# A delta-rule attention with an MLP behind it: the recurrence's small products as 128x64 tiles with two heads stacked

## The chip, the cores and the metric

The kernel runs on one core of one Trainium2 chip. Its time is the device time of one execution in microseconds (us). A core has TensorE (matrix products, PE in the profile, its weight loads PEld), VectorE (DVE), ScalarE (ACT), GpSimd (POOL), SyncE (SP, which here only issues DMAs) and 16 DMA engines. Lines named L960 and the like are lines of the kernel before, unless the text says that they are of the changed one.

## What is computed

q, k, v are [4, 8, 768, 48] and beta [4, 8, 768], all fp32: four batches, eight heads, 768 steps, 48 channels.

```python
k_n = k / (np.linalg.norm(k, axis=-1, keepdims=True) + 1e-06)
state = np.zeros((B, H, D, D))
for t in range(S):
    y[:, :, t] = einsum('bhd,bhde->bhe', q[:, :, t], state)
    v_old = einsum('bhde,bhd->bhe', state, k_n[:, :, t])
    state = state + beta_t * einsum('bhd,bhe->bhde', k_n[:, :, t], v[:, :, t] - v_old)
x = y.transpose(0, 2, 1, 3).reshape(B, S, H * D)
xn = (x - mean(x)) / sqrt(var(x) + 1e-06) * g_ln      # over the 384 channels
out = x + relu(xn @ w_ch1) @ w_ch2                     # 384 -> 1536 -> 384
```

## The kernel before, in words

The sequence is cut into 12 chunks of 64 steps (C = 64). In a chunk, the 32 pairs of batch and head are held as 16 "heads" in the free dimension and two halves of the 128 partitions (`half(e)`), two heads at a time being neighbours (`hp`, `j`: GP = 8 pairs j).

Within a chunk the recurrence is solved in closed form. `gram` and `queries` (L758) make K K^T and Q K^T, a triangular inverse is made for every head (`first_inverse` for chunk 0 by doubling on TensorE, L710 and L725; `rows_inverse` for the others, row by row on VectorE, L843 and L850, in blocks of 32 that `join` puts together with the 32x32 products L881 and L887). Then `recur(c)` does five products with the state S:

- K S (`state(p_2, kt, 0)`, L960 into PSUM tile `two`), which VectorE subtracts from v (L967);
- Q S (the same line into PSUM tile `by`);
- U = inverse times (v - K S) (`prod_u`, L994), copied by ScalarE (L996);
- the state update K^T U (`state_up`, L1011), which VectorE adds to S (L1021; in chunk 0 a ScalarE copy, L1023);
- Y, added to Q S in PSUM (`out_y`, L1001), copied by ScalarE (L1039).

Each of the five is 32 calls of nc.tensor.matmul: for each of the 8 pairs j, four calls on the four 64x64 tiles of the array, with 48 or 64 rows, 64 stationary columns (48 in the update) and 48 moving columns. Chunk 0 has no K S and Q S, and the last chunk no update. For chunk 0 the U product is L977.

Y is then normalized: in chunk 0 by VectorE's bn_stats and bn_aggr, ScalarE's square root, VectorE's reciprocal and a subtract-and-multiply (L1049 to L1061); in later chunks by `ln_act`, with sums that ScalarE accumulates. It is transposed by TensorE (L1095, chunks 0 to 2) or by VectorE and a DMA round trip through DRAM (later ones) and multiplied by g_ln into `xnt`.

The MLP follows: chunk 0 in two halves of 128 tokens (`by_halves`, L1325 and L1340, 128x128 stationary), chunks 1 to 3 with L1299 for the first product, chunks 4 to 11 with `fifteen` (15 block products instead of 18, L1220, operands combined by GpSimd), and the second product from chunk 1 on as `seven` (7 block products instead of 8, L1420). All products are fp32. The weights come as 8-byte words and are converted in the first 100 us by ScalarE, VectorE and GpSimd (L524, L529, L532, L542).

What sets the order: every step is added to a list by `add`, and `emit` issues the steps in the order of the long table ORDER; the costs, due times and priorities written beside the steps are not used by it. `in_this_order` then fixes that order on each engine, and across the DMA queues of SP and ACT. On TensorE, the recurrence of chunk c stands between dense products of the MLP of chunk c - 1 or of the one before it.

Of the kernel before, what the change touches and what calls it, by code (L numbers as in the profile page):

```python
# [16 lines left out]
C = 64  # L17
# [42 lines left out]
6 5 52 49 0 47 8 44 71 9 50 10 57 51 11 29 13 58 325 18 12 63 54 72 7 55 62 53 42 56 245 60 669 410 78 88 36 32 61 77 89 37 74 73 90 14 38 1 69 3 81  # L60
21 2 4 34 82 68 24 15 23 79 76 83 33 95 84 85 80 86 16 20 66 75 91 17 98 92 93 87 96 94 110 100 97 35 116 99 111 70 101 117 48 102 112 118 122 114 115
27 26 19 113 124 30 121 31 120 103 119 125 106 204 104 123 227 132 105 67 25 64 28 126 22 108 246 65 203 107 z 137 128 135 127 40 134 131 133 45 109
46 244 202 207 198 229 138 39 136 129 140 139 130 232 228 141 142 249 215 230 326 144 148 43 143 248 145 233 152 154 247 153 668 147 328 216 205 150
217 250 208 209 199 218 327 155 146 151 420 41 238 149 158 339 210 200 156 236 418 159 206 160 231 157 413 170 161 213 201 409 162 237 223 415 164 163
239 171 225 340 251 165 174 166 252 671 329 168 412 253 169 175 167 176 234 172 254 255 407 186 331 173 235 179 178 180 177 187 330 256 184 257 59 190
183 673 332 337 211 672 182 338 333 258 375 259 260 240 261:263 191 264 380 265 224 185 212 219 266 226 181 192 193 188 221 267 268 349 242 241 269
270 334 271 220 335 272 222 189 336 378 416 243 350 194 411 376 353 419 273 674 385 274 417 377 195 342 196 275 408 355 379 197 357 351 358 276 361
381 214 341 344 277 362 352 383 278 354 363 390 279 280 343 367 382 281 345 384 370 356 368 369 359 388 282 681 360 283 373 675 364 284 670 285 584
365 286 374 287 582 585 288 435 289 682 583 386 436 290 366 586 291 438 809 292 588 437 414 293 346 439 294 347 295 387 587 395 348 371 296 590 589
803 389 440 421 592 591 606 297 593 422 400 298 607 299 391 300 441 301:303 596 304 305 608 597 306 393 594 307 308 609 309 595 310 600 311 312 598  # L70
313 601 314 396 315 604 316 317 599 610 398 318 392 481 602 319 372 394 477 401 611 320 603 605 442 479 397 475 423 676 623 480 476 621 624 402 478
403 612 399 474 627 322 622 323 613 404 628 324 625 321 614 804 473 626 631 948 660 615 808 632 405 443 482 811 635 801 483 629 484 636 810 485 616
486 947 630 488 633 617 487 424 683 489 639 680 490 618 425 491 812 492 493 645 813 494 429 495 427 496 426 646 497 428 634 498 640 430 499 685 500
1094 647 501 432 502 684 431 637 503 433 434 504 814 648 505 815 506 444 951 507 686 508 687 649 509 445 945 1095 510 1096 511 650 946 512 1093 448
513:515 651 449 516 446 451 517 452 638 450 652 447 1209 457 453 643 458 518 1098 653 459 519 1097 460 816 641 454 654 461 520 956 677 462 455 521 944
456 688 642 955 467 678 655 522 1106 463 523 644 1099 689 524 465 1100 957 466 525 468 464 526 802 470 656 469 527 620 849 657 950 528 958 529 853 850
679 530 690 531 532 851 805 533 854 691 534 659 535 859 661 852 536 537 960 855 538:540 820 541 856 542 860 543 952 544 817 953 545:548 861 549 550
662 551 696 663 857 694 862 666 698 876 693 867 858 664 699 877 865 665 806 818 873 555 874 863 552 866 875 554 667 553 871 878 864 700 1108 868 1211
879 869 872 697 406 961 882 695 1258 870 883 560 959 954 884 658 892 885 1210 893 881 886 558 819 889 559 556 807 561 619 909 564 962 894 562 880 910
557 563 821 887 565 895 890 888 566 701 1105 896 702 692 570 911 569 899 568 897 703 567 1268 912 822 704 891 705 1267 898 900 823 917 707 913 918 914  # L80
706 963 919 1270 826 906 915 1216 571 471 824 827 708 472 828 920 709 1271 825 835 924 829 830 901 836 921 710 925 711 837 712 922 713 1217 964 838
714 831 923 1218 715 832 1205 833 572 716 717 1215 935 1101 573 926 575 902 834 927 839 965 907 903 840 936 1220 574 916 904 937 718 841 1259 905 845
719 1552 966 720 843 908 576 844 848 577 721 1109 846 842 968 847 1222 1110 938 580 1221 928 581 722 939 578 949 723 929 579 724 1554 940 1219 998 725
1551 1369 726:728 967 999 941 729 1111 943 730 969 731 1374 1556 732 1206 733 1002 1107 970 734 1370 1112 735 942 1555 736 1004 1003 1204 737 930 1368
738 971 739 1005 1223 1025 1008 931 972 1022 932 1000 740 1261 741 1557 1010 1001 742 1553 743 744 1102 1011 745 1113 973 1103 746 1564 1006 747 975
1023 1104 1009 748 1379 982 974 749 1378 1014 983 750 1373 984 751 976 752 1007 1208 1114 977 753 933 754 978 985 979 1207 1012 1015 986 755 987 756
1115 757 980 1016 989 981 758 1116 1013 759 988 1020 1028 1017 990 760 1558 934 761 1018 762 1021 763 1212 764:766 1041 767 1019 1031 768 1042 769
1032 770 1043 1122 1038 1224 1125 1024 1120 1029 1033 993 1225 1044 1034 1118 1058 1039 1045 992 1035 1026 1046 1036 1265 771 1047 1059 1037 1226 1027
772 1213 774 1266 773 1227 1030 994 1040 1060 991 1048 1260 1381 1066 1061 1117 1123 1049 1062 1119 1067 1262 1121 1050 1214 1063 1124 1068 1064 778
1051 997 779 1069 777 1052 1566 1073 1382 1070 1056 776 1074 1053 1055 775 1071 1383 1075 1065 1072 780 1367 1269 1054 1559 1084 1263 781 1076 782  # L90
1085 1264 783 1077 784 1086 995 996 1078 1126 785 1079 1384 1228 1272 1081 1380 788 786 1057 787 789 1127 2029 1087 1375 1273 1274 1128 1568 1129 1130
1563 1132 1088 1275 1229 1131 790 1080 1133 2031 1089 1134 1135 1230 1663 1280 1569 1090 1385 1136 1137 1371 1138 1278 1139 1281 1140 1091 1141 1142
1092 2033 1233 1143 1279 1372 1144 1570 1145 1082 1146 791 1235 1147 1231 1148 1242 1234 1149 1236 1276 1237 1232 1849 1243 2034 1244 1150 1286 792
1151 1277 1376 1152 1238 1296 1153 1284 1299 1386 1287 1239 1567 1297 1282 1154 1285 1674 1298 1240 794 1155 2035 1156 1290 1565 1283 1157:1159 1288
1291 1160 1245 1676 1246 1161 1305 1289 1387 1241 1303 1247 795 1390 1377 1249 793 1248 796 1250 1162 1306 1850 1302 1388 800 1294 799 1665 1300 1312
1851 1307 1163 1292 1083 1301 1164 1677 1165 1669 1308 1166 1293 1389 1167 1678 798 1313 1295 1673 1309 1304 1664 1391 1315 1253 1310 1316 1168 1311
1251 1332 1314 797 1317 1322 1169 1318 1170 1323 1171 1333 1329 1324 1680 1319 1172 2030 1334 1254 1320 1173 1335 1252 1321 1392 1174 1679 1175 1675
1176 1325 1393 1667 1177 1340 1326 1178 1845 1341 1179 1336 1571 1846 1327 1256 1342 1257 1852 1331 1337 1255 1343 1668 1180 1396 1330 1338 1181 2041
1394 1182 1183 1328 1347 1395 2142 1344 1433 1348 1345 1423 1349 1346 1444 1339 1681 1428 1397 1350 1424 1358 1399 1398 1351 1857 1400 1184 1359 1421
1662 1352 1401 1560 1185 1405 1425 2144 1406 1402 1186 1445 1435 1360 1407 1187 1449 1438 1353 1561 1188 1442 1403 1361 1189 1434 1408 1452 1562 1450  # L100
1429 1409 1404 1362 1190 1430 1410 1446 1451 1426 1412 1363 1411 1427 1448 1572 1364 1453 1437 1413 1447 1191 1439 1454 1573 1192 1436 1193 1440 1456
1670 1194 1431 1455 1195 1458 1441 1574 1457 1432 1461 2028 1459 1416 1671 1422 1465 1460 1414 1354 1462 1463 1417 1672 1666 1471 1464 1415 1355 1468
1466 2043 1357 1682 1443 1469 1198 1196 1472 1477 1356 1473 1200 1474 1853 1467 1478 1859 2045 1480 1576 1479 1475 2040 1581 1470 1496 1365 1481 1483
1497 1578 1484 1482 1199 1498 1419 1490 1485 1197 1420 1499 1476 1366 1486 1491 1500 1487 1201 1510 1501 1738 1492 1580 1502 1683 1582 1488 1493 1523
1579 1489 1516 1511 1418 1577 1524 1503 1583 1494 1517 1504 1203 1684 1495 1525 1861 1505 1518 1512 1202 1526 1860 1519 1854 1728 1506 1727 1527 1520
# [95 lines left out]
def kernel(  # L201
# [20 lines left out]
    FT = DFF // 128  # L222
    GH = 2 * H
    NP = H // 2
    TURNED = 4
    LNPE = 2
    GP = 2 * NP
    FROM, LATER = 4, 6
# [1421 lines left out]
```

## Time and profile before

| | us |
|---|---|
| median of 3 runs | 511.74 (510.79 to 512.89) |
| the profiled execution | 511.19 |
| its span, first to last instruction | 509.5 |
| TensorE busy | 488.8 |
| VectorE, ScalarE, GpSimd busy | 352.1, 249.9, 276.3 |
| L1420, L1220, L1299 as a share of the chain that ended last | 31%, 22%, 9% |
| the small products L960, L994, L1001, L1011 as a share of that chain | 9% in all |

A group's row in the profile gives line, engine, operation, output<-inputs, shapes and count, then busy time in us and the mean ns of one instruction. Matmuls overlap in the pipeline, so the mean of one is longer than the distance between two starts; the chain that ended last, in order of time, gives what each piece adds: start in us, length in us, line and count. A fp32 matmul call shows as two records.

### The profile page before, as it was taken

To read this page: it belongs to the slowest core of one execution; us is meant where nothing else is said; L and a number is where in the kernel's file an instruction comes from. 1 tells how busy PE (TensorE), PEld (TensorE's weight loads), DVE (VectorE), ACT (ScalarE), POOL (GpSimd) and SP (SyncE) were. 2 spreads that over 40 slices of the span, in tenths; PEclk is the share of its full clock that TensorE was granted. 3 is DMA by queue.
4 is the path that set the end of the run, shared out by engine and by line. 5 is a ranking of instruction groups with operands and counts; after the bars stand their busy time and mean duration, and the time that the engine had idled before them with its cause. 6 is when DMAs were issued, how large, how long until landed. Compare 5 with 4: busy or idle time off the path is not lost.

```text
span 509.5 us, 22177 instructions
## 1 busy us (share of the span) xinstructions
PE 488.8 (96%) x9608; PEld 446.4 (88%) x9608; DVE 352.1 (69%) x776; ACT 249.9 (49%) x613; POOL 276.3 (54%) x432
## 2 busy tenths in 40 slices
PE   6866999999999999999999999999999999999996
PEld 3655888689898898899999999999999999999995
DVE  4679887896799638798548998559999456243251
ACT  4688663652464436427334745336554247463230
POOL 5255518416864497549784553581552851455643
PEclk8697599999999999999999999999999999999999
DMA  9987767777365777374874346644354430211001
GB/s 162 326 159 207 176 178 117 104 161 105 61 97 120 188 105 130 75 109 148 168 90 60 83 72 180 124 60 78 73 96 109 100 61 10 66 48 46 18 16 31
DMA packets 196097, 54.99 MB, mean 108 GB/s; under 512 B 186076, under 2 KB 189404, under 8 KB 196000
## 3 DMA queue, kind: packets, MB, share of 16 engines
q1 hardware_dynamic: 189920, 40.58, 41.9%
q10 hardware_dynamic: 3872, 9.83, 5.9%
q0 software_dynamic: 2208, 3.17, 4.3%
q8 instruction: 75, 1.23, 1.0%
q14 instruction: 22, 0.18, 0.1%
HBM read 36.64 MB, written 16.91 MB: 105 GB/s over the span
## 4 chain that ended last, share of the span: by engine, by line
PE 89%; ACT 3%; DVE 3%; DMA 2%; issue 2%; POOL 1%; ACTq 0%; SPq 0%; DVEq 0%; POOLq 0%
PE f L1420 31%; PE f L1220 22%; PE f L1299 9%; PE two L758 4%; PE f L1325 3%; PE f L1340 3%; PE by L1001 3%; PE two L960 2%; PE by L960 2%; PE two L994 2%; PE two L1011 2%; ACT xt L669 1%; DMA gd<-gsb 1%; DMA kr<-in_k_dram 1%; PE by L887 1%
## 5 line engine op out<-in xcount | busy, mean ns | idle before, releaser
L1407 POOL TENSOR_TENSOR h_all<-h_all 128x256 f32<-128x256 f32 x123 | 90.2, 742 | 132.9 <-PE f L1420 103.8
L1420 PE MATMUL f<-w_sb,h_all 128*128 128x192 f32 x492 | 109.6, 331 | 0.0
L1420 PE MATMUL f<-words,h_all 128*128 128x192 f32 x396 | 86.1, 330 | 0.2 <-POOL h_all L1407 0.2
L1420 PEld LDWEIGHTS f<-w_sb,h_all 128*128 128x128 f32 x492 | 81.9, 190 | 1.6
L1240 DVE TENSOR_TENSOR h_all<-h_all,f 128x512 f32<-128x512 f32 x96 | 63.6, 683 | 19.6 <-PE f L1220 15.6
L850 DVE TENSOR_TENSOR xb<-xb,tmp 128x87 f32<-128x87 f32 (+21 forms) x186 | 74.0, 398 | 4.5
L843 DVE TENSOR_TENSOR tmp<-xb,gb 128x87 f32<-128x87 f32 (+21 forms) x186 | 72.3, 389 | 4.6
L1420 PEld LDWEIGHTS f<-words,h_all 128*128 128x128 f32 x396 | 66.8, 190 | 1.6 <-POOL h_all L1407 0.9
L349 POOL DMA_DIRECT2D tb<-in_k_dram x64 | 41.9, 660 | 14.0 <-DVE kt L738 10.0
L1299 PE MATMUL f<-xnt,w_sb 128*128 128x256 f32 x216 | 49.4, 382 | 0.0
L1242 ACT ACTIVATE h_all<-h_all 128x512 f32<-128x512 f32 x48 | 28.9, 623 | 40.7 <-DVE h_all L1240 40.3
L1299 PEld LDWEIGHTS f<-xnt,w_sb 128*128 128x128 f32 x216 | 40.3, 190 | 5.6
L1236 ACT COPY h_all<-f 128x512 f32<-128x512 f32 x48 | 26.5, 588 | 31.5 <-PE f L1220 20.4
L1438 DVE TENSOR_TENSOR o<-f,x 128x192 f32<-128x192 f32 x33 | 11.6, 355 | 36.8 <-PE f L1420 27.0
L1220 PE MATMUL f<-words,w_sb 128*128 128x128 f32 x256 | 32.5, 277 | 0.1
L1220 PEld LDWEIGHTS f<-words,w_sb 128*128 128x128 f32 x256 | 30.3, 192 | 0.4 <-issue 0.2
L1308 ACT ACTIVATE h_all<-f 128x256 f32<-128x256 f32 x36 | 13.4, 381 | 30.0 <-PE f L1299 29.9
L542 POOL TENSOR_TENSOR w_sb<-words 128x768 uint32<-128x768 uint32 (+1 forms) x11 | 15.3, 1395 | 22.7 <-DMA words<-in_moe_w_ch_dram 8.3
L1220 PE MATMUL f<-xnt,w_sb 128*128 128x128 f32 x192 | 25.3, 275 | 0.0
L1220 PEld LDWEIGHTS f<-xnt,w_sb 128*128 128x128 f32 x192 | 23.9, 192 | 0.1
L1325 PEld LDWEIGHTS f<-xnt,w_sb 128*128 128x128 f32 x144 | 18.9, 198 | 3.5 <-ACT h_all L1333 0.7
L996 ACT COPY u<-two 128x768 f32<-128x768 f32 x11 | 8.8, 799 | 26.4 <-PE two L994 26.3
(246 smaller groups left out, 958.2 us busy)
## 6 DMA issues: line engine op xcount, KB each, us to landing
words<-in_moe_w_ch_dram ACTq DMA_DIRECT2D x10, 768.0 KB, 5.4
gd<-gsb SPq DMA_DIRECT2D x11, 512.0 KB
v<-in_v_dram SPq DMA_DIRECT2D x24, 192.0 KB, 4.4
kr<-in_k_dram SPq DMA_DIRECT2D x46, 96.0 KB, 3.2
out_dram<-o SPq DMA_DIRECT2D x44, 96.0 KB, 2.3
xld<-xlt SPq DMA_DIRECT2D x9, 384.0 KB
xnt<-xld SPq DMA_DIRECT2D x36, 96.0 KB, 3.4
gb<-gd SPq DMA_DIRECT2D x44, 64.0 KB, 3.5
```

The source lines that it names most:

```text
L349: add(eng, cost, lambda: QUEUE[eng].dma_start(out=out_, in_=in_), r, w, bulk=n * ns / 16e3, **kw)
L758: nc.tensor.matmul(pair[hp][half(e ^ (hp & n)), (g * NP + j) * C : (g * NP + j + 1) * C], kt[drows(hp), l], rt[drows(hp), i],)
L843: lambda j=j, n=n, w=w, t=t: nc.vector.tensor_tensor(out=t, in0=xv[:, 0:n, j : j + 1].to_broadcast([np_, n, w]), in1=gv[:, j : j + 1, j + ...
L850: "DVE", dve(n * w), lambda t=t, rest=rest: nc.vector.tensor_tensor(out=rest, in0=rest, in1=t, op=ALU.subtract),
L1220: nc.tensor.matmul(wide(p[:, 128 * n : 128 * n + 128]), w[n // 2][:, n % 2 * 128 : n % 2 * 128 + 128], r, start=start and n == 0, stop=Tru ...
L1236: add("ACT", act(512), lambda: nc.scalar.copy(o, p), pk, ok)
L1240: add("DVE", dve(512), lambda: nc.vector.tensor_tensor(out=o, in0=o, in1=p, op=op), pk, ok)
L1242: add("ACT", act(512), lambda: nc.scalar.activation(o, o, ACTF.Relu), [], ok)
L1299: nc.tensor.matmul(p[:, 0:TOK], w1_sb[:, t, f * 128 : (f + 1) * 128], xnt[:, t], start=(t == 0), stop=(t == KC - 1))
L1325: nc.tensor.matmul(p[:, 0:128], w1_sb[:, t, f * 128 : (f + 1) * 128], xnt[:, t, cols], start=(t == 0), stop=(t == KC - 1))
L1407: add(eng, cost, lambda: e.tensor_tensor(out=out_, in0=x, in1=y, op=op), r, w, port=2 if eng == "Pool" else 1, pr=-2)
L1420: lambda f=f, t=start and f == 0: nc.tensor.matmul(p[:, 0:D2], lhs(f), rhs[:, f], start=t, stop=(f == F2 - 1), skip_group_check=True),
```

## The change

K S (of chunks 2 to 11), Q S, U, Y and the state update (of chunks 1 to 10) become 16 calls each, with all 128 rows (two heads stacked along the rows that are summed), 64 stationary columns (48 in the update) and 96 moving columns. The moving operand, the state or U, is kept block-diagonal: `s_all` and `u_all` are [128, 8, 4, 48], cleared once by GpSimd, and `picks` takes the 96 columns of one pair. For each pair j two calls write the two halves of PSUM's partitions.

```diff
-    s_all = sb("s_all", [128, 2, GP, D])
+    s_all = sb("s_all", [128, GP, 4, D])
-    kraws = [sb(f"kr{i}", [128, GH * DP]) for i in range(3)]
+    kraws = [sb(f"kr{i}", [128, GH * DP]) for i in range(2)]
-    us = sb("u", [128, GH, D])
+    u_all = sb("u", [128, GP, 4, D])
...
+    def natural(ps):
+        return ps[:, :, 0 : NP * 2 * D].rearrange("p g (j n d) -> p g j n d", n=2, d=D)
+
+    def picks(t, x):
+
+        return t[:, :, 1:3] if x else t[:, :, ::3]
...
+            def state(dst, src):
+                for j in range(GP):
+                    for e in range(2):
+                        nc.tensor.matmul(
+                            dst[half(e), j // NP, j % NP], src[:, e * GP + j], picks(s_all, e)[:, j],
+                            start=(j % NP == 0), stop=False, skip_group_check=True,
+                        )
...
+                    for n in range(2):
+                        nc.tensor.matmul(n_2[half(n), j // NP, j % NP], xt[:, 2 * j + n], picks(u_all, n)[:, j])
...
+        def add_y():
+            for j in range(GP):
+                for e in range(2):
+                    nc.tensor.matmul(
+                        n_y[half(e), j // NP, j % NP], pt[:, 2 * j + e], picks(u_all, e)[:, j], start=False, stop=True, skip_group_check=True
+                    )
...
+        def add_up():
+            for j in range(GP):
+                for hp in range(2):
                     h0 = 2 * j + hp
                     nc.tensor.matmul(
+                        n_2[drows(hp), j // NP, j % NP], kp[:, h0 * DP : h0 * DP + D], u_all[:, j, 2 * hp : 2 * hp + 2]
                     )
```

The evictions are cut in two, because the blocks lie at different places of the two halves: v - K S and the state's sum (VectorE) and the copy of U (ScalarE) are each two instructions of 64 or 48 partitions, and chunk 0's copy of the state too.

```diff
+            for e in range(2):
+                o = u_all[half(e), :, e::2].rearrange(to, g=2)
+                add(
+                    "DVE", dve(768),
+                    lambda e=e, o=o, v_j=v_j, ks=ks: nc.vector.tensor_tensor(out=o, in0=v_j[half(e)], in1=ks[half(e)], op=ALU.subtract),
+                    TWO + vk + ["u_zero"], [("ub", e)], **kw,
+                )
...
+            for n in range(2):
+                o = u_all.rearrange("p (g j) n d -> p g j n d", g=2)[half(n), :, :, n::2]
+                add("ACT", act(768), lambda o=o, n=n: nc.scalar.copy(o, n_2[half(n)]), TWO + ["u_zero"], [("ub", n)], **kw)
```

Chunk 0 is normalized by `ln_act` too, but only its mean is subtracted (on VectorE) ahead of the transposes; the factor 1/std is multiplied in behind the second product of its MLP:

```diff
-                lambda o=o, p=p, g=g: nc.vector.tensor_tensor(out=o, in0=p[:, 0:DM], in1=x[:, g], op=ALU.add),
-                pk + [("x", 0, g)], o_keys(g), pr=-5,
+                lambda o=o, p=p, g=g: nc.vector.scalar_tensor_tensor(
+                    out=o, in0=p[:, 0:DM], scalar=rstd[:, 0, g : g + 1], in1=x[:, g], op0=ALU.mult, op1=ALU.add
+                ),
+                pk + [("x", 0, g), ("ln", 0, g)], o_keys(g), pr=-5,
```

In `first_inverse` the copies behind levels 2 to 5 move only the half of the columns that changed, and level 5 multiplies and merges only half of them:

```diff
-                o, i = xt[po, hs], src(int(n > 0), pi)
-                add("ACT", act(256), lambda o=o, i=i: nc.scalar.copy(o, i), r[int(n > 0)], [xtk[g][n]], **kw)
+                o, i = col3(xt[po, hs], m, 1), col3(src(int(n > 0), pi), m, 1)
+                add("ACT", act(128 if m >= LEAST else 256), lambda o=o, i=i: nc.scalar.copy(o, i), r[int(n > 0)], [xtk[g][n]], **kw)
```

Memory is shared to make room: `es` lies in `xlt`, chunk 0's `us` in `xnts[1]`, and there are two raw buffers of k instead of three. From chunk 2 on (TURNED = 2 instead of 4) the heads of the upper half are held in their own order, so k of chunks 2 and 3 is loaded padded for its transposes, raw k of chunk 2 later in its step, the diagonal that `norms` reads comes in three DMAs instead of two, beta_b in 20 instead of 8 and beta_f in three instead of two. Each `join` stands in the step of its own chunk. ORDER is another table: the steps are reordered throughout.

## The prediction, before the changed kernel was run

> **What bounds the kernel now.** First the page's busy times and slices, then the chain that ended last, then that chain piece by piece in a late stretch, and the groups by shape.
>
> ```profile
> PE 488.8 (96%) x9608; PEld 446.4 (88%) x9608; DVE 352.1 (69%) x776; ACT 249.9 (49%) x613; POOL 276.3 (54%) x432
> ...
> PE   6866999999999999999999999999999999999996
> ...
> PEclk8697599999999999999999999999999999999999
> ...
> PE 89%; ACT 3%; DVE 3%; DMA 2%; issue 2%; POOL 1%; ACTq 0%; SPq 0%; DVEq 0%; POOLq 0%
> ```
>
> TensorE is busy in 96% of the span and makes 89% of the chain. Only the first four or five slices (12.7 us each) have gaps, at a granted clock of 0.5 to 0.9; from about 53 us on there is always another matmul. So two questions set the time: how much TensorE time the change adds or removes after 53 us, and how soon the first 53 us end. A stretch of the chain gives the prices (start, length, both us):
>
> ```profile
> 290.72 1.08 PE two L960 x64
> 291.80 0.93 PE by L960 x64
> 292.73 3.12 PE f L1420 x18
> 295.85 1.08 PE two L994 x64
> 296.93 3.12 PE f L1420 x18
> 300.05 1.08 PE by L1001 x64
> 301.13 0.72 PE two L1011 x64
> 301.85 0.52 PE f L1420 x2
> 302.37 0.89 PE f L1220 x8
> ...
> 312.27 1.09 PE two L758 x64
> ```
>
> The 32 calls of a small product show as 64 records, and so do the 6 calls of a `prod` of `seven` as 12: each fp32 matmul runs as two passes. Read: a small product behind another takes 0.93 us, behind dense work 1.08; the state update behind another takes 0.72; and L758, whose moving operand has 64 columns instead of 48, costs the same 1.09. So the moving width is not what limits a small product; the stationary width is (64 columns: 0.93; 48 columns in L1011: 0.72).
>
> **Two rules from these rows.** Per pass, dense: in the same stretch 22 passes of L1420 take 3.77 us and 18 take 3.12, so one of 192 moving columns takes 162.5 ns. Near 116 and 157 us the chain has 42 passes of L1299 (256 columns) in 9.26 us and 18 in 4.08: 215.8 ns. The difference is 0.833 ns per moving column, plus 2.5. Small: 64 passes in 0.934 us are 4 in 58.3 ns, and 64 in 0.72 us 4 in 45.0. The difference is again 0.833 ns per (stationary) column, plus 5. The 128-column dense pass fits that: 8 in 0.89 us, 111 ns, against 0.833 x 128 + 5 = 111.7. I read this as: the four 64x64 tiles work side by side, and in each a pass takes the longer of its weight load, 0.833 W + 5, and its stream, 0.833 N + 2.5. At N = 64 the stream would need 55.8, just below 58.3, as L758 shows.
>
> **Part 1: the 53 products.** K S of chunks 2 to 11 (10), Q S, U and Y of 1 to 11 (11 each), state update of 1 to 10 (10). Each goes from 64 passes on four tiles to 16 calls, 32 passes, on two tiles of 128x64: 53 x 32 = 1,696 matmul records fewer. Stationary columns stay 64 (48 in the update), moving columns go from 48 to 96. Per tile 16 passes remain, as before, but each now needs max(58.3, 0.833 x 96 + 2.5 = 82.5): 16 x 82.5 = 1.32 us. Half the moving columns multiply zeros; the array pays for them.
> - K S, Q S, U, Y: 1.32 - 0.934 = +0.386, 43 times: +16.6 us.
> - Update: 1.32 - 0.72 = +0.60, 10 times: +6.0 us.
> - Entering and leaving a run of small products costs 1.08 + 3.12 - 18 x 0.1625 - 0.934 = 0.34 us. By the built order of the changed program the dense stretches between such runs go from 78 to 77, so I count no change.
>
> Sum +22.6. No row has a 128x64 pass. Below: the weight load alone limits (as for all small rows), 16 x 58.3 and 16 x 45 are today's prices, change 0. Lower still: tiles stream at twice the dense rate (rival 2). Above: the two tiles do not overlap, 32 x 82.5 = 2.64 us, +92.6. I take 1.32: it is the dense rows' price per column with the overlap of the small rows.
>
> The Trainium skill (TensorE: Matmul & The Clock Gate, Back-to-back issue gap) gives an issue floor of about 25 ns from start to start however few columns; by it 64 passes would take 1.6 us and 32 passes 0.8, which speaks for the change. The trace disagrees: 14.6 ns a pass here, 11.3 in L1011. So counting instructions is not the price.
>
> **Part 2: evictions.** V - K S and the state add (VectorE, 128x768, 0.944 and 0.942 us) and the copy of U (ScalarE, 0.799) become two of 64 or 48 partitions, 768 elements each. ScalarE's 64x256 copy costs 366 ns and the 128x256 one 371: partitions don't matter, so each half costs the whole. VectorE +21 x 0.94 = 19.8 us (352 to 372), ScalarE +12 x 0.80 = 9.6. Cover: dense work. In the built order at least 2.0 us of it stands between U and Y where 1.6 + semaphores are needed, and about 2.3 or more, most of it dense and some small, between K S and U, needing 1.9. Cost 0; with the cover short by half a microsecond per chunk, +5.
>
> **Part 3: start.** Chunk 0's `bn_stats` 0.56, `bn_aggr` 0.17, Sqrt 0.30, reciprocal 0.15 leave the way to the first MLP; a mean (about 0.2, as the 196 ns accumulator read) and the same 0.47 subtraction stay. In the trace x is ready at 53.11 and normalized at 56.39; it should take 1 us. But TensorE runs other work in between (transposes, U and Y of the second half at half clock), of which the built order moves two transposes ahead and Y behind the first dense matmuls: some 1.3 us less before L1325, which starts at 61.28. In the inverse, ScalarE's copies of the levels 2 to 5 halve (0.37 to about 0.27 us, 3 per group and level: -2.4 us on an engine busy 9.5 of 10 us between 30 and 50), and two copy_predicated shrink from 0.73 to about 0.45. I take -3 us. Against it stand two Pool memsets of 128x1536 (1.43 each by the 0.955 of 128x1024; Pool's weight conversions are on the chain here), one more beta_f issue (0.71), and 12 more beta_b issues on SP at about 0.6 us ahead of nothing but later loads. Range of the start: -6 to +4.
>
> **Part 4: the rest.** One more diagonal load per chunk (SP, 11 x 0.6 us over the run), k of chunk 2 loaded once more in another layout, joins beside their own chunk (the same 22 groups of 32x32), `es` in `xlt`, `us` in `xnt`, two raw buffers: SP idles in long waits for its producers (52 us for the output sums alone) and the raw load of a chunk now waits for the update two chunks back, still a chunk (30 us) ahead. The pad of two matmuls dropped in the start fell into idle time. Cost 0; if a load is late the wait lands on the join or the update, at most a few us.
>
> **Sum.** The profiled execution took 511.19 us (span 509.5 and 1.7 around it), 0.55 under the median 511.74. 511.2 + 22.6 - 3 = 530.8.
>
> **Rivals.**
> 1. Only the weight load limits a tile: products unchanged, 511.2 - 3 = 508.2. For it: no small row is limited by its stream. Against: 82.5 exceeds 58.3 unless a tile streams 1.4 times faster than any dense row. 0.07.
> 2. The other side. "4 passes in 58.3" can also be read as two tiles at a time, each pass 29.2 = 0.417 W + 2.5, a tile moving columns at twice the dense rate. Then a pair takes 0.417 x 96 + 2.5 = 42.5 and a product 16 x 42.5 = 0.68: -0.254 x 43 - 0.04 x 10 = -11.3, giving 496.9. It decides where the product falls below 0.93 us, a pitch of 29.2 ns over its 32 passes. For it: the rows fit the rates equally well. Against: the dense 128-column pass fits the first reading (111.7; the second gives 109.2, a thin margin), and the mean weight load grows from 135 ns (64 columns, L960) to 190 (128, L1420), 0.86 ns per column, the first reading's rate. 0.12.
> 3. The two column tiles take turns: 511.2 + 92.6 - 3 = 600.8. Against: the four tiles now overlap in columns too. 0.04. The Trainium skill (same page, The mechanism) says weight loads pass running matmuls only where the row groups differ, and both new tiles use all rows; by its rule a pass would be 58.3 + 82.5 and a product 4.5 us, some +190 us. The trace disagrees for dense work, whose loads (190 ns, all rows) hide entirely in a 162.5 ns pitch.
> 4. The start slips: the Pool memsets hold the weight conversions, and the halves stall TensorE: +4 and +5 instead of -3, 543. 0.04.
>
> **How the numbers follow.** Forecast 0.73, its own range 525 to 542 (start -6 to +4, run overhead and evictions a few us more). The range 505 to 542 adds rival 1 and leaves out rivals 2, 3 and most of 4, about 0.2. Half a per cent, 2.6 us, is about what a measurement of this kernel can tell from no change: slower 0.81 (forecast, 3, 4), same 0.03, faster 0.16 (2, most of 1).
>
> **What would show it.** In the changed profile, a wide product behind another at 1.32 us (L997, L1048, L1067, L1081 alike, the update no cheaper than the others), against 0.93, 0.68 or 2.64; 7,908 matmul records on TensorE; still 96% busy without new gaps after 60 us; the first L1387 near 58 us. The forecast is wrong if the 32 passes of a product start within 0.93 us.

## The result and the profile after

The changed kernel takes 533.31 us (median; 533.18 to 533.82), the kernel before beside it 511.4: a ratio of 1.0426, 95% interval 1.0401 to 1.0450. It is 4.3% slower. The forecast was 530.8. The profiled execution took 533.82 us, with a span of 532.1.

The page of the changed kernel: busy times (share of the span, instructions), the busy tenths and granted clock of TensorE in 40 slices (13.3 us each), and the chain's shares.

```profile
PE 510.3 (96%) x7908; PEld 466.8 (88%) x7908; DVE 368.1 (69%) x792; ACT 260.8 (49%) x633; POOL 284.1 (53%) x435
...
PE   6876899999999999999999999999999999999996
...
PEclk9579799999999999999999999999999999999999
...
PE 83%; DVE 5%; SPq 4%; ACT 2%; issue 2%; DMA 2%; POOL 0%; ACTq 0%; DVEq 0%; POOLq 0%
```

TensorE has 1,700 records fewer and is busy 21.5 us longer. It still has work without a break from the sixth slice on, at the same clock. VectorE's 16 and ScalarE's 11 us more are busy time of engines that still stand idle a third and a half of the span. So the loss must lie in what each record takes, and the chain that ended last shows it (start, length, engine and line; L997 is K S and Q S, L1048 U, L1067 Y, L1081 the state update, L1484 the dense `seven`):

```profile
273.79 1.47 PE by L997 x32
275.26 1.32 PE two L1048 x32
276.58 3.12 PE f L1484 x18
279.70 1.47 PE by L1067 x32
281.17 1.32 PE two L1081 x32
```

A wide product behind another takes 1.32 us where it took 0.93, and the update 1.32 where it took 0.72. The dense 18 passes beside them still take 3.12. Behind dense work it is 1.47: the head of a run is 0.15 more, as before (1.08 against 0.93).

The same sum over the whole trace: from the start of each TensorE record to the next one's, from the first matmul of the MLP to the end, K S and Q S went from 22.58 to 31.21 us, U from 11.81 to 15.87, Y from 11.37 to 15.33, the update from 8.73 to 14.01. That is 54.5 to 76.4, 21.9 us more, of a difference of 22.6 between the two profiled executions. (In the chain of the kernel before, these products make 11%, the sum of 2.3, 2.2, 2.2, 2.5 and 2.0, and not the 9% of the table above.) The rest nearly cancels. The first matmul of the MLP starts at 59.11 us instead of 61.21 (2.1 gained), and half of chunk 0's Y now stands behind that point (0.61 lost). The timelines, first of the kernel before, then of the changed one (start, length, engine and line):

```profile
61.21 2.33 PE L1325 MATMUL f<-xnt,w_sb 128*128 128x128 f32 x12
```

```profile
59.11 1.60 PE L1387 MATMUL f<-xnt,w_sb 128*128 128x128 f32 x12
60.65 0.68 PE L1059 MATMUL by<-xnt,pt 64*64 64x48 f32 x32
```

TensorE has 1.97 us of gaps after 56 us instead of 0.39 (1.6 lost). These four add up to 22.0 of the 22.6 us; the other 0.6 is spread over other lines. Nearly all of the gaps are in four waits (engine and line that waits, and for whom; total us, times, longest):

```profile
PE f L1282 <- DVE o L1502: 0.6, 1, 0.6
PE two L1005 <- DVE pt L813: 0.6, 1, 0.6
PE f L1387 <- ACT h_all L1395: 0.4, 1, 0.4
PE f L1484 <- POOL h_all L1471: 0.2, 1, 0.2
```

The last of them is in the kernel before too; the other three are new, and end at 247.97, 76.15 and 66.07 us. None is at a wide product.

### The profile page after: what moved, and what is told of

It reads as the page before. It is cut to its first block, busy times and chain, and to the rows that moved or that the text cites. A ratio compares the mean times of both kernels' runs of the same rounds, so it can differ in the third digit from the quotient of the medians.

```text
span 532.1 us, 18836 instructions
## 1 busy us (share of the span) xinstructions
PE 510.3 (96%) x7908; PEld 466.8 (88%) x7908; DVE 368.1 (69%) x792; ACT 260.8 (49%) x633; POOL 284.1 (53%) x435
## 3 DMA queue, kind: packets, MB, share of 16 engines
q8 instruction: 62, 1.02, 0.8%
## 4 chain that ended last, share of the span: by engine, by line
PE 83%; DVE 5%; SPq 4%; ACT 2%; issue 2%; DMA 2%; POOL 0%; ACTq 0%; DVEq 0%; POOLq 0%
PE f L1484 26%; PE f L1282 21%; PE f L1361 7%; SPq L360 4%; PE by L1067 3%; PE two L782 3%; PE two L1048 3%; PE by L997 3%; PE f L1402 3%; PE two L1081 3%; PE two L997 2%; PE f L1387 2%; DVE tmp L867 1%; PE f L579 1%; DVE xb L874 1%
## 5 line engine op out<-in xcount | busy, mean ns | idle before, releaser
L1484 PE MATMUL f<-w_sb,h_all 128*128 128x192 f32 x492 | 108.6, 330 | 0.0
L1484 PE MATMUL f<-words,h_all 128*128 128x192 f32 x396 | 87.3, 331 | 0.2 <-POOL h_all L1471 0.2
L1484 PEld LDWEIGHTS f<-w_sb,h_all 128*128 128x128 f32 x492 | 82.5, 190 | 2.1 <-DVE o L1502 0.2
L867 DVE TENSOR_TENSOR tmp<-xb,gb 128x87 f32<-128x87 f32 (+21 forms) x186 | 74.9, 403 | 4.6
L874 DVE TENSOR_TENSOR xb<-xb,tmp 128x87 f32<-128x87 f32 (+21 forms) x186 | 71.7, 385 | 4.9
L1484 PEld LDWEIGHTS f<-words,h_all 128*128 128x128 f32 x396 | 66.8, 190 | 2.0 <-ACT h_all L1304 0.5
L1361 PEld LDWEIGHTS f<-xnt,w_sb 128*128 128x128 f32 x216 | 40.0, 190 | 6.2 <-ACT xnt L1172 0.4
L1098 DVE TENSOR_TENSOR s_all<-s_all,two 48x768 f32<-48x768 f32 x20 | 19.0, 949 | 16.0 <-PE two L1081 9.1
L1054 ACT COPY u<-two 64x768 f32<-64x768 f32 x22 | 17.5, 794 | 21.2 <-PE two L1048 21.1
L1020 DVE TENSOR_TENSOR u<-v,two 64x768 f32<-64x768 f32 x22 | 20.9, 950 | 9.9 <-PE two L997 5.6
L1502 POOL TENSOR_TENSOR o<-o,words 128x192 f32<-128x192 f32 x22 | 13.1, 607 | 21.1 <-DVE words L1502 15.6
```

The lines of the kernel that those rows point to most:

```text
L867: lambda j=j, n=n, w=w, t=t: nc.vector.tensor_tensor(out=t, in0=xv[:, 0:n, j : j + 1].to_broadcast([np_, n, w]), in1=gv[:, j : j + 1, j + ...
L874: "DVE", dve(n * w), lambda t=t, rest=rest: nc.vector.tensor_tensor(out=rest, in0=rest, in1=t, op=ALU.subtract),
L1361: nc.tensor.matmul(p[:, 0:TOK], w1_sb[:, t, f * 128 : (f + 1) * 128], xnt[:, t], start=(t == 0), stop=(t == KC - 1))
L1484: lambda f=f, t=start and f == 0: nc.tensor.matmul(p[:, 0:D2], lhs(f), rhs[:, f], start=t, stop=(f == F2 - 1), skip_group_check=True),
L1502: lambda: e.tensor_tensor(out=out_, in0=a, in1=b_, op=ALU.add), r, w, pr=pr,
```

## The experiments

Theory A is that of the prediction: on each tile of the array a pass takes the longer of its weight load, 0.833 ns per stationary column + 5, and its stream, 0.833 ns per moving column + 2.5, and two 128x64 tiles work side by side.

### One part undone: the products back on 64x64 tiles

```diff
-                    for e in range(2):
+                    for m, e in hp_e:
                         nc.tensor.matmul(
-                            dst[half(e), j // NP, j % NP], src[:, e * GP + j], picks(s_all, e)[:, j],
+                            dst[half(e), m, j], src[drows(m), e * GP + j], s_all[drows(m), j, 2 * m + (e ^ m)],
```

U, Y and the update likewise; the views of the evictions follow.

> The changed kernel with its wide products taken back to 32 calls on four 64x64 tiles each, every call reading the one 48-column block of the block-diagonal operand that is not zero. Evictions in halves, the new start and the new order stay. Theory A (the stream of the 96 moving columns is the whole cost): each product falls from 1.32 to 0.93 us and the update to 0.72, 22.6 us less than the changed kernel's 533.3, so 510.7; the start, 2 us earlier than in the kernel before, and small stalls of about the same size behind it leave it within 1 us of the kernel before. Theory B (part of the loss is in what else changed: halved evictions, order, loads): above 514. Theory C (the start is worth its 2 us and the new stalls belong to the wide products): 508 to 509.5.

Measured: 511.91 us, a ratio of 1.0 to the kernel before (0.9979 to 1.0022). In its chain:

```profile
291.50 1.08 PE by L997 x64
292.58 0.93 PE two L1048 x64
298.91 1.08 PE by L1067 x64
299.99 0.72 PE two L1081 x64
```

The old prices are back, and with them the old time. So everything else in the change, taken together, is worth nothing that this comparison can tell (its interval is 0.2% to either side, 1.1 us), and the products are the whole loss. Theory A's 510.7 is missed by 1.2 us; B and C are out. In this trace the first matmul of the MLP starts at 58.19, 3 us before that of the kernel before, and 2.6 us of gaps behind 56 us take the gain back. The longest, 0.94 us at 422 us, lies in the middle of a U product and waits for nothing that the profile shows.

### What sets the price: moving columns, stationary columns

Three runs change only the shape of the wide calls.

```diff
-    dst[half(e), j // NP, j % NP], src[:, e * GP + j], picks(s_all, e)[:, j],
+    dst[half(e), j // NP, j % NP, :, 0:24], src[:, e * GP + j], picks(s_all, e)[:, j, :, 0:24],
```

> The changed kernel with the 96 moving columns of a wide product cut to 48 (24 of each of the two blocks); the other 24 columns of every head are left out of the recurrence. 128 rows, 64 stationary columns, 16 calls as they were. Theory A: a tile's pass is the longer of weight load (58.3 ns, update 45) and stream (42.5), so a product takes 0.93 us and the update 0.72: 533.3 - 22.6 = 510.7. Rival D (a call on 128 rows costs 82.5 ns whatever it moves, by its weights or its issue): 533. Rival E (only the stream counts, at 0.833 ns a column per tile, and the 128x64 tiles hide their weight loads wholly): 0.68 us a product, 533.3 - 53 x 0.64 = 499.

The same with 0:40:

> The changed kernel with 80 moving columns per wide call instead of 96 (40 of each block; the last 8 columns of every head are left out of the recurrence). Theory A, which needs a slope now that 48 and 96 fit it: a pass takes 0.833 x 80 + 2.5 = 69.2 ns, a product 1.107 us, 53 x 0.213 = 11.3 us less than the changed kernel's 533.3: 522. Rival H (a stream costs in steps, or anything above 64 columns pays for 96): 533. Rival I (anything below 96 is free down to the weight load): 510.

And the stationary operand cut instead:

```diff
-    dst[half(e), j // NP, j % NP], src[:, e * GP + j], picks(s_all, e)[:, j],
+    dst[quad(2 * e), j // NP, j % NP], src[:, e * GP + j, 0:BK], picks(s_all, e)[:, j],
```

> The changed kernel with the stationary columns of every wide call cut from 64 (48 in the update) to 32; the other output rows are left out. 96 moving columns as they were. Theory A: the stream (82.5 ns) stays the longer part, 1.32 us a product, 533. Rival F (weight load and stream add up, 58.3 + 24 or the like): a pass loses 0.833 x 32 = 27 ns, a product 0.43 us, 533.3 - 43 x 0.43 - 10 x 0.21 = 513. Rival D in the form that 128-row weights are what costs: also less, by up to the same 20 us.

Measured: 508.62 us with 48 moving columns (ratio 0.9924, 0.9901 to 0.9948), 521.25 with 80 (1.0196, 1.0172 to 1.0219), 531.91 with 32 stationary columns (1.0381, 1.0354 to 1.0407). Their chains, U and the update behind another product, first with 48 moving columns:

```profile
292.32 0.93 PE two L1048 x32
...
299.72 0.72 PE two L1081 x32
```

With 80:

```profile
268.58 1.11 PE two L1048 x32
...
274.07 1.10 PE two L1081 x32
```

With 96 moving and 32 stationary columns:

```profile
305.00 1.32 PE two L1048 x32
...
313.16 1.32 PE two L1081 x32
```

Read as nanoseconds per pass on a tile (16 passes): 58.3 and 45.0 at 48 columns, where the weight load is the longer part and the update's 48 stationary columns still show. At 80 the two meet at 69, where the stream is longer, and at 96 both are 82.5. Halving the stationary columns at 96 changes nothing. Rival D (a fixed price of a 128-row call), E (stream alone: 42.5 at 48 columns), F (the two add up), H and I (steps) are all out. The run with 48 columns is 2 us under the sum's 510.7: its first matmul of the MLP starts at 57.22, 1.9 earlier than in the profiled changed kernel, whose start it shares, and its wide products are 23.1 us shorter than there instead of 22.6. So most of the miss is the spread of the start.

### Do the two tiles overlap, and how

```diff
-                for j in range(GP):
-                    for e in range(2):
+                for e in range(2):
+                    for j in range(GP):
```

> The changed kernel with the two loops of each wide product exchanged: first the eight calls on one column half of the array, then the eight on the other. Theory A (a tile streams at the dense rate, and two tiles overlap only because neighbouring calls go to different tiles): the halves run one after the other, a product takes up to 32 x 82.5 = 2.64 us, 53 x 1.32 = 70 us more, 603. Rival G (one stream feeds both tiles, so a pass takes 41 ns on whichever tile): no change, 533.

Measured: 582.73 us (ratio 1.1374, 1.1343 to 1.1405). A Q S product and the U behind it, in the chain:

```profile
296.16 2.26 PE by L997 x29
298.42 0.06 PE two L1048
298.48 0.03 PE by L997
...
298.67 2.09 PE two L1048 x29
300.76 3.12 PE f L1484 x18
```

Rival G is out: on one tile a pass takes the whole 82.5 ns (the starts lie 82 or 83 apart for twelve passes in a row). But the two products together take 4.60 us and not 5.28, for L1048 begins while L997 still has passes to do. In the starts of the records around a change of side, the first pass of the new side starts 6 ns after the 13th of the old one's 16; seven intervals there take 304 ns instead of 577. One change of side saves 0.27 us, 3.3 passes. The timeline shows the order around the change from L997 to L1048 (records that start in a row on one line are merged):

```profile
297.76 0.66 PE L997 MATMUL by<-s_all,qt 128*64 128x96 f32 x6
298.18 0.30 PE L1048 MATMUL two<-u,xt 128*64 128x96 f32 x1
298.26 0.25 PE L997 MATMUL by<-s_all,qt 128*64 128x96 f32 x1
298.31 0.25 PE L1048 MATMUL two<-u,xt 128*64 128x96 f32 x1
298.34 0.25 PE L997 MATMUL by<-s_all,qt 128*64 128x96 f32 x1
```

In the program all of L997's calls stand ahead of L1048's, and yet three passes of L997 start behind the first one of L1048. So TensorE starts passes on a free tile a few passes ahead. How many, the next two runs ask:

```diff
+    RUNS = [(j + i, e) for j in range(0, GP, 2) for e in range(2) for i in range(2)]
...
-                for j in range(GP):
-                    for e in range(2):
+                for j, e in RUNS:
```

> The changed kernel with each wide product's calls in runs of two per column half (two calls, four passes, on one half, then two on the other, and so on). In the run with eight calls per half the passes stood 82.5 ns apart except around each change of side, where four passes of the next half ran beside the last four of the one before. If TensorE starts passes on a free tile up to about four passes ahead, runs of two calls are hidden wholly: 533, a product still 1.32 us. If it looks only one call ahead, half the overlap goes: about 2.0 us a product, 565 to 570.

> The same with runs of four calls (eight passes) per half. With a look of four passes ahead, each change of side hides four of eight passes: a product has four runs of eight passes, 660 ns each, three changes inside it and one to its neighbour that save about 330 ns each: 2.64 - 1.2 = 1.4 to 1.65 us, 538 to 551. With no look ahead it would be the eight-call run's 583 or more.

Measured: 534.49 us for runs of two calls (ratio 1.0451, 1.0432 to 1.0469) and 552.22 for runs of four (1.0797, 1.0778 to 1.0816). In the chains, two first, then four:

```profile
305.80 1.52 PE by L997 x32
307.32 1.32 PE two L1047 x32
```

```profile
315.61 1.72 PE by L997 x29
...
317.58 1.55 PE two L1047 x29
```

Four passes on one side before the other side comes cost nothing inside a product and 0.05 us at its head (1.52 against 1.47). With eight, the two products take 3.52 us from 315.61 on; the price of the run with eight calls per side, 2 x 2.64 + 0.13 - 3 x 0.27 = 4.60 (the 0.13 is what its head leaves over), becomes with seven changes of side 2 x 2.64 + 0.13 - 7 x 0.27 = 3.52. My bound for it was a little low, since I had taken a change to hide four passes where it hides 3.3.

### The evictions

The kernel before with its evictions cut in halves, nothing else:

```diff
-            add("DVE", dve(768), lambda: nc.vector.tensor_tensor(out=v_j, in0=v_j, in1=p_2, op=ALU.subtract), TWO, vk, **kw)
+            def minus_ks():
+                for e in range(2):
+                    nc.vector.tensor_tensor(out=v_j[half(e)], in0=v_j[half(e)], in1=p_2[half(e)], op=ALU.subtract)
+            add("DVE", dve(768), minus_ks, TWO, vk, **kw)
```

> The kernel before with its evictions alone cut into halves of 64 partitions (v - K S, the state's sum, the copy of U and chunk 0's copy of the state), the products as they were. Forecast: VectorE is busy about 20 us more and ScalarE 9 to 10 more, and the time does not move: 511 to 512.5. Rival (the halves stall TensorE between K S, U and Y): up to half a microsecond in each of 11 chunks, 517.

Measured: 516.79 us, 5.3 more than the kernel before (ratio 1.0106, 1.0086 to 1.0125). The rival was right here. Groups of this run (busy us, mean ns; then the idle time ahead):

```profile
L970 DVE TENSOR_TENSOR v<-v,two 64x768 f32<-64x768 f32 x22 | 20.8, 946 | 6.7 <-DMA ksum<-gd 5.6 <-PE two L960 0.9
L1032 DVE TENSOR_TENSOR s_all<-s_all,two 64x768 f32<-64x768 f32 x20 | 18.9, 946 | 0.8 <-PE two L1019 0.6
```

And what TensorE waited for after 60 us:

```profile
PE two L758 <- DVE s_all L1032: 1.4, 3, 0.6
PE f L1436 <- DVE o L1454: 1.0, 2, 0.5
```

A half costs the whole (946 ns against 944), as forecast. But the order of the kernel before has no room for it: the next product that writes `two` waits for the state's sum, and dense products wait for output sums behind it in VectorE's queue. After 56 us TensorE's gaps grow from 0.39 to 4.25 us, and the first matmul of the MLP starts 0.85 later, at 62.06. No U and no Y waits for its own eviction, which is where the rival had put the stall. The changed kernel's own order does have the room: no wait of a wide product for an eviction appears in it.

To see what the halves and GpSimd's clearings cost there, the products on 64x64 tiles again, with whole evictions and operands without zero blocks:

```diff
-    s_all = sb("s_all", [128, GP, 4, D])
+    s_all = sb("s_all", [128, 2, GP, D])
-    u_all = sb("u", [128, GP, 4, D])
+    u_all = sb("u", [128, 2, GP, D])
-    c_pool(lambda: nc.gpsimd.memset(s_all, 0.0), 1.4, ["s_zero"], t0=12.0)
-    c_pool(lambda: nc.gpsimd.memset(u_all, 0.0), 1.4, ["u_zero"], t0=24.0)
```

> The changed kernel's start, order and loads, with the products taken back to 32 calls on 64x64 tiles and the evictions taken back to one instruction each (state and U without zero blocks, so GpSimd's two clearings of 1.4 us are gone too). If the halved evictions and the clearings cost what little is lost besides the products (a wait of 0.9 us of one U product for its halves in the run with halves, and small stalls): 508.5 to 510, that is 2 to 3 us under that run's 511.9 and faster than the kernel before by 0.3 to 0.6%. If the evictions are hidden, as forecast, and the start's gain is eaten by the two or three new stalls around 65, 75 and 235 us, which stay: 511 to 512, the same as before.

Measured: 511.2 us, ratio 0.9995 (0.9977 to 1.0012); the second alternative held. The MLP starts at 55.42 here, and yet the time is the same within its interval: 3.8 us of gaps follow after 56 us. The three new waits of the changed kernel are among them (0.6, 0.6 and 0.4 us, at the same steps), with whole evictions too, so the halves are not their cause. That the clearings are gone is not shown to be the reason of the early start: the run with runs of four calls per side has them and starts at 55.37, and the other seven runs with the changed kernel's start lie between 57.2 and 59.1.

### The start

The changed kernel with chunk 0's 1/std put back ahead of the transposes (in the order, root and reciprocal move up behind the subtraction):

```diff
+            if not c:
+                def by_std(g=g, rs=rs):
+                    nc.vector.reciprocal(rs, rs)
+                    nc.vector.tensor_scalar(out=xlns[g], in0=xlns[g], scalar1=rs, scalar2=None, op0=ALU.mult)
+                add("DVE", 0.6, by_std, [], ck + [("xln", g)], **kw)
```

> The changed kernel with chunk 0's 1/std put back ahead of its transposes: ScalarE's squares, root and VectorE's reciprocal follow the subtraction at once, VectorE multiplies the factor in, and the last sum is a plain add again. Products wide. The chain from x to the transposes grows by about 0.53 + 0.19 + 0.28 + 0.15 + 0.47 = 1.6 us per half, the halves partly one behind the other. If the start waits for that chain: 535 to 536.5, and the first matmul of the MLP near 61 us. If the chain stands beside other waits of the start (inverse, weights): 533.3.

Measured: 537.93 us (ratio 1.0524, 1.0501 to 1.0547), 4.6 over the changed kernel's median, in the two profiled executions 3.5. The MLP starts at 62.24. TensorE's longest waits in the start:

```profile
PE two L1166 <- DVE xln L983: 4.1, 1, 4.1
PE f L785 <- issue: 1.6, 1, 1.6
```

L1166 is the transpose. It waits 4.1 us for the normalized x; in the changed kernel that wait is 1.37. So the start does wait for this chain, and moving 1/std behind the MLP is worth some 3 us of it. (The 1.6 of "issue" has no cause that the profile shows, and may be part of the 4.6.) The start here is also 1.0 later than in the kernel before. No run takes the halved copies of the inverse or the reordering back by themselves, so a gain from them is not shown.

### An attempt to keep that gain

The last two kernels take the run with 64x64 tiles and whole evictions, and move steps away from the new waits.

```diff
+    moved = {360: 361, 451: 452, 589: 601, 1438: 1384}
```

Step 361 is issued right behind step 360, and so on; the second of the two kernels leaves out the third pair.

> The run with products on 64x64 tiles, whole evictions and no clearings, with four steps moved in the order to take out what TensorE waited for behind the start: the second half's subtraction of the mean (0.57 us at 71) and the mask of chunk 1's Q K^T product (0.59 at 72) go ahead of row steps of the inverse on VectorE, a second MLP product goes between two first ones (0.37 at 62), and an output sum goes ahead of a row step on VectorE (0.62 at 235). If these waits are what is left of the start's gain: 511.2 - 2.1 = 509, faster than both kernels by about 0.45%. If others take their place: 510.5 to 511.5.

> The run before it with four moved steps came out at 514.3 instead of 509: the four waits were mostly gone, but TensorE waited 2.9 us at 74 us for a weight tile, whose words had landed 12.2 us after their load was issued and then passed ScalarE, VectorE and GpSimd. This run leaves out one of the four moves, that of the second MLP product between two first ones, and keeps the three on VectorE. If that move set ScalarE's evictions, and with them the conversions and the next weight load, back: the wait goes and the time is 509 to 510. If the three moves on VectorE hold up the conversion of the words, or the weights' arrival is simply the bound once the start is this early: 513 to 514.5 again.

Measured: 514.28 (ratio 1.0058, 1.0046 to 1.0070) and 513.81 (1.0040, 1.0023 to 1.0057). Both slower than what they started from. The first of them, TensorE, VectorE and ScalarE between 67 and 77 us:

```profile
69.13 1.23 DVE L816 TENSOR_TENSOR pt<-two,pmask 128x1024 f32<-128x1024 f32 x1 [1.89 <-PE two L785]
...
73.94 1.48 DVE L543 TENSOR_SCALAR words<-words 128x768 uint32<-128x768 uint32 x3
```

```profile
76.80 1.65 PE L1402 MATMUL f<-w_sb,h_all 128*128 128x384 f32 x2 [2.91 <-POOL w_sb L556]
```

The mask that I had moved up waits 1.89 us for its product L785, and the row steps and the conversion of the weight words queue behind it on VectorE: the conversion starts at 73.94 instead of 70.84. GpSimd's half of it follows, and TensorE waits 2.9 us for the weight tile. The words themselves also landed later, at 71.7 instead of 69.4. The second run has the same wait (2.5 us), so the move that it leaves out was not the cause. How much of it is the load and how much VectorE is not settled. None of the kernels here that compute the whole recurrence is measurably faster than the kernel before.

## Why the prediction was right, point by point

- **The two rules.** Right in every size tried: 58.3 and 45.0 ns at 48 moving columns, 69 at 80, 82.5 at 96 whatever the stationary width, and 82.5 for single-file passes on one tile. The rate was taken from dense rows with 128 stationary columns and carried to another tile shape; that step held.
- **Part 1.** Forecast +22.6, measured +21.9 in the trace, and 21.4 between the medians with the wide products and with them undone (533.31 - 511.91). Most of the 0.7 too much is in the update (+5.3 for the +6.0 forecast). The head of a run is unchanged. The update costs as much as the others, as said.
- **Part 2.** Right that a half costs the whole (950 and 794 ns; in the kernel before with split evictions VectorE is busy 18.2 us more), and right at 0 for the changed order. The fallback "with the cover short by half a microsecond per chunk, +5" has the size that the kernel before shows when its evictions are split, +5.3, but that is partly luck: there the gram products and the dense products wait, not U and Y. The cover is a property of the order, so the value could only be read from the built order of the changed program.
- **Part 3.** Forecast -3 and the first matmul of the MLP near 58 us. In the eight runs that share this start it begins at 55.4 to 59.1, 57.8 on average, against 61.21 in the one trace of the kernel before. What was left out is what comes behind: 0.6 us of Y that I had counted as gone had only moved behind that point, and gaps behind it, most of them the new waits of part 4, take 1.6. This -3 is the term that was mis-sized: at the end of the run the gain is gone, as the run with the products undone shows (ratio 1.0). Between 530.8 and the 533.8 of the profiled execution this makes 3.1 us (0.9 of the start, 0.6 of Y and 1.6 of gaps); the products, 0.7 below their forecast, and the 0.6 that is spread over other lines nearly cancel. The clearings on GpSimd, which I left in the range, could not be told from the spread of the start.
- **Part 4.** Not tested by itself. The run that undoes the products alone holds parts 2, 3 and 4 together and comes out at nothing. The sign "without new gaps after 60 us" did not hold: the three new waits, 0.4 to 0.6 us each, stand there. They stay with whole evictions, and they stay when the start is later than in the kernel before (the run with 1/std ahead), so they come with the rest of the change (order, shared memory, loads), for which this part had put 0. Which of its steps makes them is open.
- **Rivals.** 1 (weight load only, 508.2) and 2 (twice the dense rate, 496.9) fall with the 1.32 us; 2 also with the single-file passes at 82.5. 3 (the tiles take turns) is false as long as the calls alternate, and seven tenths true when they don't: +49 us of the +70 that no overlap at all would cost. 4 (late start, stalls by the halves) didn't happen in the changed order; in the order before, its stalls do. The Trainium skill (TensorE: Matmul & The Clock Gate, The mechanism), in its list of what overlaps, lets weight loads pass running matmuls only across row groups. The trace disagrees with that: both tiles use all rows here, and passes on one tile still follow at 82.5 ns, the time of the stream alone.

## What to carry to other kernels

Price a small product by passes per tile times the longer of weight load and stream, not by the number of instructions: stacking two heads along the rows with a block-diagonal moving operand halves the calls and the number of tiles together, so each tile keeps its 16 passes, and every pass streams twice the columns. By these rules it never saves TensorE time. It costs nothing only while the weight load is still the longer of the two: up to 67 moving columns for 64 stationary ones, an estimate from the two rules; with 48, the 128x64 tiles take the 0.93 us of the 64x64 ones. Calls on different tiles overlap only if they stand within about four passes of each other in the program. And before a step is moved up on an engine that takes its steps in the program's order, look at what it waits for: everything behind it will wait too.

## What the hardware showed that I had not expected

TensorE does not start its passes strictly in the order of the program: with eight calls on one column half and then eight on the other, passes of the second half start beside the last four of the first, and one change of side hides 0.27 us (3.3 passes of 82.5 ns). With four passes per side the overlap is complete (1.32 us a product behind another). I read this as a look ahead in its queue; how it is made, no run here shows.

Waits of 0.4 to 0.9 us in the middle of a small product, put down to "issue", appear after 62 us in all four traces that have the new order and 64x64 products, and in none of the eight with wide ones. (The 1.6 us of the run with 1/std ahead ends at 61 us.) The programs with 64x64 products move more instructions (1.23 MB against 1.02 in the queue of instructions), but the kernel before moves as many and has no such wait. Their cause stays open.
